# Nine identity products between the first scores and the first weighted sums of a fused attention and long-convolution kernel

## The chip, the cores and the metric

The kernel runs on one core of a Trainium2 chip. Such a core has TensorE (matrix products, which land in PSUM), VectorE and ScalarE (elementwise work; both read PSUM), GpSimd, and SyncE, which here only issues transfers. The traces call these engines PE (PEld for its weight loads), DVE, ACT, POOL and SP. The metric is the device time of the program in microseconds; a profiled execution also gives a span, from the first to the last instruction.

## What is computed

```python
B, S, D = 8, 3136, 256           # z has 64 columns
scores = (1 / S) * (z @ z.T)     # per batch, symmetric
attn = np.maximum(scores, 0) ** 2
x = u * (attn @ v)
proj = x @ w_proj
x1, x2, x3 = proj[..., :D], proj[..., D:2*D], proj[..., 2*D:]
x2_conv = irfft(rfft(x2, axis=1) * rfft(filter_fft, axis=0), n=S, axis=1)
y = x1 * x2_conv * x3
out = y @ w_out
```

## The kernel before

Each batch's 3136 rows are cut into seven chunks of 256 to 512 columns, and into 25 row tiles of up to 128 rows. For each chunk TensorE makes the scores of a few tiles at a time (`score_mm`, a unit), VectorE or ScalarE takes their positive part out of PSUM into R_t (`relu`, lines 1956 and 1958) and squares it into A_t in bf16 (`sq`, lines 1965 and 1967; a few units of the first batch land in buffers named conv_in_t and spec_in_t instead), and TensorE adds the unit's weighted sum of v's rows to the chunk's sum (`weigh`). Since the scores are symmetric, some units are sent through a transposing transfer into M_t and reused for another chunk. When a chunk's sum is whole, VectorE multiplies it by u (line 2012), TensorE projects it, and the convolution runs as two stages of small Fourier products through DRAM. All this is interleaved over the batches.

PSUM is held as four pairs of banks, `ps_t[0]` to `ps_t[3]`; in the order of instructions they are `ps_s_139` to `ps_s_142`. A chunk's running sum keeps a pair until it is whole; scores take one for each unit.

The order is written out by hand. `ORDER` is a string of two-character codes; `Plan.go` takes them one by one and emits the task of that number on its engine. `ENGINES` says which engine takes an elementwise task, `BANKS` which pair a task takes. A code past the last task is no task but a fill, into the pair that the code names:

```python
if k >= len(every):
    self.fill(k - len(every))

def filler():
    p = take_pair()
    for h in range(2):
        i = ident[rows_of(h), :]
        matmul(p[:, h, :], i, i.unsqueeze(1).to_broadcast([N1, 4, P]), start=True, stop=True)
```

A fill thus issues two products of 64 rows of the identity with a repeated copy of the same rows, one in the upper and one in the lower half of the array's rows, each writing one bank of the pair. Nobody reads their result. The kernel before has such fills near its end, and eight identity products over all 128 rows at its start, ahead of everything else on TensorE.

The opening, in which the change lies, makes batch 0's z ready and begins chunk 0. z arrives in pieces of 4, 8 and 13 tiles. Each piece is cast to bf16 twice side by side (`cast`, into xT_t, lines 619 on ScalarE and 623 on VectorE), transposed on TensorE against the identity (`turn`, line 558, into PSUM), and copied out into zT_t (`back`, line 623). After the first piece come the first two score units, each of two tiles with one product for a tile; after the second come the first weighted sums into pair 0, the next scores, and so on. Pair 0 holds the first piece's transposes until VectorE has copied them out, and from the first weighted sum on the running sum of chunk 0. GpSimd meanwhile starts the transfers of v and u, and VectorE also builds the tables of the Fourier stages (percol, gs_t).

Of the kernel before, what the change touches and what calls it, by code (L numbers as in the profile page):

```python
# [11 lines left out]
P = 128  # L12
# [43 lines left out]
    "r}r~2e3Y2f363ks03i3Z3l2g2u372h2w3as13r3B3ss23vs33w2p3b2i2q3c3m2js42k3t3d3n3e3x3f3C2l0c2v0es50d3Q3y3R"
    "s60f3$0g3D3%3)s73j3*s83&3q3Ss93+3;3p3u3<3#3o3(3z3:3=3!3E3,sA3F494G4AsB3>4H3/0lsCsD4B4I0msE0nsF4N4J4C"
    "4K4OsG0o4R4D3-4S3?4E3G4TsH4P444X4UsI4Y3H3T4F3I4b3U454L4csJ4M4Z4i4W4d4msK4n4j0p4e4V3.0q4Q0r4o4a4f4vsL"
    "4k0s4h4p3J4wsM4l4g4x3K3@3L3V4q4?sN464ssO4@3[sP3]50sQ4t514u4[4y520t57473^4]584^sR0usS0v533_4z4_4{594|"
    "0w4}5D4r3{5M4:5EsT4;4~5NsUsV5FsW565O5h555A5l5i5s5B5C5msX5G545JsY5t5wsZ5j5L5#3M5n5P5x5K3N5usa5o5$sb5y"  # L60
    "5H3O5k5)5q5*sc5Q5-3P5%5r5.3|4<5e5&5v5f4=5+3}5(5z3~5<sd485=4!5Ise5/5!5>4#sf4$5?5^0x5p0y5,5_0z5}sg5@5:"
    "5;5{5~5]0!7n7r607osh7vsi7ssjsk7w4%7psl5[5|7t4&7x7z61404(7!sm41sn427%627q7&7u7#437k7)7lso7*7.7(4)7y7/"
    "7$7?7+4*7@sp4>4+7_7,7-7{7:5R7~5Ssq5T7[0#7;sr7<807>7|7]84ss85815U0$5V7^5W0%88827}86st898D8a0&su8E8b83"
    "7=8f8Asv8F878c8m8Bsw8n8C8g8Gsx8o0(8q8h8d0)sy0*8e8r8i0+sz8j8xs!8H8ys#0,8#8k8s8$8V8l8W4,638z0;s$4-644."
    "8t8p8%8u8+s%654/8:8w8,8&8;8v8(5Xs&5Y8-665Z5g8[s(8)8<8]8!8|s)8}8^8=9K8*9L8>8/8~9S8.679T8@0-689Ms*0.0/"
    "8_0<s+0=s,0:5a8{5b8I8X5c0>909U0?5d690@8J9V9Y8K6A9Zs-7m9Ws.9N6B9a0{9O9b91s/9c9P8Y9i9Q9j9F9d9n9Gs:9t8?"
    "9o9R9u9y9k9e9X9f8L9ps;9z6C8M9v9h9q8N9r6D0[6Es<9w9m9!0]9)A1s=6F9*A29s9#0^9$s>9+0_0|9xs?9g0}0~8O109(A3"
    "9l8P928Q8ZAB9Hs@A4A56G9,ACAF93AGs[ADAM6Ts]94s^AH8RANs_9I8SA69-8TAIAQs{9%A7AR9{959|98AOAS96A8AX97A9AJ"
    "AY998UATAUs|9&9AAb9J6HAcAA6I9.AZs}AjAE6JAk6M9/6K6jAL6N6LA)AP9:A*s~6RAd6Ot09BAl6SA:AKAe9CAWAft1A;6P6U"
    "AVt26Q6VAa9Dt3A+6ZAhA[t46W6at59}9;6XA]Ai6b6c6Y9<6dAm9=6ht6A<t76eA,6iA=A{An6zA>A-A|A.A^6k6fB2A#A/9EA$"  # L70
    "6gB66l9~t8B7t9B36pA?Ag6m6qA@A}tAB4BD6nA~9>B06otBBE6r9?B8tCA09@BHA_BFB9BIBQBAB5tDBRB1BJBCBlBvBGA%BmBw"
    "BKBB6sBLBP6t6x9[6yA&tEBS9]tF6u9^B!AoBNB#tGBntHBT6v9_BxB)ApBo6wBOtIB*BqAqB$tJB<tKBMBrB=BUBsB%BtB&C8tL"
    "C9tM6!B>BiB+BuBj6#BzB,B(CACCB-tNCJCD6$6(BytO6)CKB;Ar6%tPCEB/6+As6&6,tQCFBpAtAuCLB:CNtRAvCO6-6:AwB?6*"
    "6.CBtS6;6/CSCHtTB@CT6<CPCICUC5A(B.Ax6=CVCXCWAyCYCMAztUC6CbCQCZCgCR6>ChCnCctVCoCaBVCiCdCrtWCpA!EECsCj"
    "BWCkCeEFBXtXCGBYCfCtEIEGBZEJtYEMCmBaENCqCuBbEKtZ6?EOtaBc6}EQBkB[BdtbERtcClB]tdB^teESEUEXEVEHELCvEPEY"
    "EcEWEBBetfECEdEjBfETEkEZtgthBgEeEaEotiEpB}ElEsEfEbBhEgEtB~EiEmEnC0EuExEq6@E#6[tjEy6]76ErEvtkE$E)B_E*"
    "tlEzB{F1EhC7EwB|E%6^tmE+F2F66_tnF76{E&C1E!C2E(F8F3Cw6|6~toC370F9CxFA71E,7ECyFDtpC4FEFHF4tqFICzE-F5FF"
    "C!trFOC#E{C$E|tsFPFBFSFCFTFJFGC%72C&EDFQFKFZ73FLFaFN74FettFftuFUC(75FRC)E.C*FbFVFlFMFWE/FmtvE:FY77Fn"
    "twC+FgFq78FrFd79E>FXFhFiFkFsE?E}7A7ME@F:Fp7BF;E~txF]7CtyF^tzF<F~t!FcG0t#G2FtG3F_7FE;7GG1t$Fo7HF{E<F|"
    "G4F=F0F>Fu7DG9G5t%GAF?E=F+GE7UF,F@GFGKFjGLE[t&GB7IG6F[GGGME]7Jt(E^7KGHGNt)GIt*GPGXGQF}FvE_G8GYGRG7Fw"  # L80
    "Gut+Fx7NGSt,GTGDGv7OG&GCGJG(GO7PFyGwt-GZG+7cFzG)GxG<C,GyGWF!t.G=Gat/G,G>C^7QG@7RF-G[t:7SGzGVG-t;F#Gb"
    "G]G}G.F.G!G/F$G~G^G#GpF/G_G$F%GqGcH0H2GdH3GUt<GeC-G%C.7LH4t=HAC<HBG*C/H57Tt>H6t?C=C:HXC;t@HYC_C>G;C{"
    "G?DAC?HeC[C@HCt[C]G|HfD0t]H8C|H1D1D3Grt^D4C}G:HlF&C~t_Hm7VF(D57WH9G{F)7XGfHDD6HZ7YD7HpD2GgHgHnt{7Zt|"
    "HqHht}GhHi7aHaHrDQHvt~HEHwHsHzHbHcH!F*HxHSGiHTGsHFH#H)GjHdH*H7GtH$HGH%u0GkHHH-Htu1H.D8H+7bHjD9H@HkH["
    "DBHuH/Hou2DCICH]DGH:u3H=H;u4DHIDu5DJH&HyDKDD7dH(HUDEIE7eDIH,7fGlIMu6IFINDFGmIRH?GnDLHVu7ISH^IOu8IXGo"
# [2021 lines left out]
```

## Time and profile before

| | |
|---|---|
| median of 3 runs | 942.79 us (938.34, 942.79, 945.0) |
| the profiled execution | 942.77 us, its span 940.9 us |
| mean granted clock of TensorE | 0.997 |
| TensorE, VectorE, ScalarE, GpSimd busy | 914.0, 838.7, 819.6, 247.6 us |
| moved by the DMA engines | 170.70 MB, mean 181 GB/s |

Products on TensorE are pipelined and their ends are modelled, so two products that overlap in the two row halves show as two durations of the same time. Idle time of an engine is put down to what ended it. A line such as L553 is that of a helper through which every product goes, so the tile names tell products apart: `ps_s<-zT_t` are scores, `ps_s<-A_t,v_t` weighted sums, `ps_s<-ident,xT_t` transposes of z, and `ps_s<-ident` the eight products at the start or a fill.

### The profile page before, as it was taken

To read this page: it belongs to the slowest core of one execution; us is meant where nothing else is said; L and a number is where in the kernel's file an instruction comes from. 1 tells how busy PE (TensorE), PEld (TensorE's weight loads), DVE (VectorE), ACT (ScalarE), POOL (GpSimd) and SP (SyncE) were. 2 spreads that over 40 slices of the span, in tenths; PEclk is the share of its full clock that TensorE was granted. 3 is DMA by queue.
4 is the path that set the end of the run, shared out by engine and by line. 5 is a ranking of instruction groups with operands and counts; after the bars stand their busy time and mean duration, and the time that the engine had idled before them with its cause. 6 is when DMAs were issued, how large, how long until landed. Compare 5 with 4: busy or idle time off the path is not lost.

```text
span 940.9 us, 30306 instructions
## 1 busy us (share of the span) xinstructions
PE 914.0 (97%) x12425; PEld 555.4 (59%) x12425; DVE 838.7 (89%) x1117; ACT 819.6 (87%) x952; POOL 247.6 (26%) x585
## 2 busy tenths in 40 slices
...
DMA  9899899989999789998999989998999979898867
GB/s 158 155 176 163 141 156 197 185 144 173 169 218 201 151 190 168 206 200 146 192 173 212 177 160 189 178 223 149 200 167 208 224 128 202 202 205 140 207 193 232
DMA packets 331644, 170.70 MB, mean 181 GB/s; under 512 B 242887, under 2 KB 307143, under 8 KB 331505
## 3 DMA queue, kind: packets, MB, share of 16 engines
...
q10 hardware_dynamic: 712, 1.66, 0.6%
q14 instruction: 43, 0.34, 0.2%
...
## 4 chain that ended last, share of the span: by engine, by line
PE 83%; ACT 5%; DMA 5%; DVE 5%; issue 2%; SPq 0%; POOL 0%; DVEq 0%; ACTq 0%; POOLq 0%
PE ps_s L553 82%; DMA M_t<-A_t 3%; ACT R_t L1956 2%; DVE xh L1394 1%; DVE A_t L1967 1%; DMA zn_t<-in_z_dram 1%; ACT A_t L1965 1%; DVE xT_t L2012 1%; DMA A_t<-spec 0%; ACT xh L619 0%; DMA spec<-uT_t 0%; ACT ost_t L619 0%; ACT s_t L619 0%; DVE gs_t L623 0%; ACT R_t L619 0%
## 5 line engine op out<-in xcount | busy, mean ns | idle before, releaser
L553 PE MATMUL ps_s<-A_t,v_t 64*128 64x512 bf16 (+5 forms) x4766 | 515.7, 352 | 1.1 <-DVE A_t L1967 1.0
L553 PEld LDWEIGHTS <-v_t 64*128 64x128 bf16 (+1 forms) x6528 | 305.8, 98 | 185.9 <-PE ps_s L553 19.2
L1956 ACT ACTIVATE R_t<-ps_s 128x1024 f32<-128x1024 f32 (+3 forms) x359 | 336.8, 961 | 50.4 <-PE ps_s L553 47.2
L1965 ACT ACTIVATE A_t<-R_t 128x1024 bf16<-128x1024 f32 (+2 forms) x281 | 271.8, 992 | 12.0 <-DVE R_t L1958 4.9
L1967 DVE SCALAR_TENSOR_TENSOR A_t<-R_t 128x1024 bf16<-128x1024 f32 (+3 forms) x211 | 233.6, 1123 | 17.6 <-ACT R_t L1956 10.3
L553 PE MATMUL ps_s<-zT_t 64*128 64x512 bf16 (+5 forms) x1186 | 191.4, 352 | 4.4 <-DVE gate_t L1293 1.7
L1958 DVE TENSOR_SCALAR R_t<-ps_s 128x1024 f32<-128x1024 f32 (+4 forms) x153 | 170.3, 1124 | 23.7 <-PE ps_s L553 13.3
L676 POOL COPY tick<-A_t 1x1 bf16<-1x1 bf16 x159 | 54.3, 341 | 426.0 <-ACT A_t L1965 262.0
L553 PE MATMUL ps_s<-xT_t,wp 64*128 64x512 bf16 (+3 forms) x976 | 124.3, 352 | 0.5 <-DVE R_t L1958 0.4
L553 PEld LDWEIGHTS <-zT_t 64*128 64x128 bf16 (+1 forms) x1219 | 68.9, 97 | 52.8 <-issue 9.8
L553 PE MATMUL ps_s<-M_t,v_t 64*128 64x512 bf16 (+4 forms) x860 | 96.6, 353 | 1.8 <-DMA M_t<-A_t 1.7
L619 ACT ACTIVATE x_t<-ps_s 128x1024 bf16<-128x1024 f32 (+3 forms) x75 | 69.4, 927 | 20.9 <-PE ps_s L553 18.1
L1394 DVE TENSOR_TENSOR xh<-xh,H 128x1024 bf16<-128x1024 bf16 x120 | 81.8, 685 | 2.9 <-ACT xh L619 2.0
L1293 DVE TENSOR_TENSOR gate_t<-ps_s,x_t 128x512 bf16<-128x512 f32 (+2 forms) x112 | 64.5, 617 | 12.4 <-PE ps_s L553 10.3
L2012 DVE TENSOR_TENSOR xT_t<-ps_s,uT_t 128x512 bf16<-128x512 f32 (+2 forms) x112 | 64.0, 614 | 6.5 <-PE ps_s L553 6.1
L1499 DVE TENSOR_TENSOR yT_t<-ps_s,gate_t 128x1024 bf16<-128x1024 f32 (+2 forms) x53 | 56.9, 1078 | 12.9 <-PE ps_s L553 11.7
L553 PEld LDWEIGHTS <-wp 64*128 64x128 bf16 (+1 forms) x976 | 47.8, 96 | 30.0 <-PE ps_s L553 2.0
L553 PE MATMUL ps_s<-wp,xT_t 64*128 64x256 bf16 (+2 forms) x944 | 64.0, 266 | 0.1
L553 PE MATMUL ps_s<-wo,yT_t 64*128 64x256 bf16 (+2 forms) x904 | 62.3, 266 | 1.0 <-DVE yT_t L1499 0.5
L662 POOL DMA_DIRECT2D un_t<-in_u_dram x112 | 58.1, 519 | 18.5 <-issue 16.0
L688 POOL DMA_DIRECT2D v_t<-in_v_dram x112 | 58.4, 525 | 13.6 <-issue 10.3
L553 PEld LDWEIGHTS <-xT_t 64*128 64x128 bf16 (+1 forms) x944 | 43.5, 97 | 19.1 <-issue 0.6
...
## 6 DMA issues: line engine op xcount, KB each, us to landing
...
```

The costliest lines, as they stand in the source:

```text
L553: got = nc.tensor.matmul(o, *args, **kw)
L619: got = nc.scalar.activation(out_, in_, AF.Copy)
L662: nc.gpsimd.dma_start(out=t[ds(j * N1, N1), lo - t0 : hi - t0, :], in_=x[:, n2 : n2 + hi - lo, :])
L688: nc.gpsimd.dma_start(out=t[ds(j * N1, N1), ds(v_at(a), (b - a) * D)], in_=r[:, n2 + a - lo : n2 + b - lo, :].rearrange("p t d -> p (t d)"),)
L1293: has_read(nc.vector.tensor_tensor(o[:, :, ::-1] if h == 0 else o, p, x, ALU.mult), p)
L1394: nc.vector.tensor_tensor(x[:, 1 - i], x[:, 0], h, ALU.mult)
L1499: has_read(nc.vector.tensor_tensor(yb["y"][:, :, 0:w], p, gates[b, c][:, :, 0:w], ALU.mult), p)
L1956: has_read(nc.scalar.activation(r, p, AF.Relu), p)
L1958: has_read(nc.vector.tensor_single_scalar(r, p, 0.0, ALU.max), p)
L1965: nc.scalar.activation(a, r, AF.Square, scale=1.0 / float(S))
L1967: nc.vector.scalar_tensor_tensor(a, r, inv_s2, r, ALU.mult, ALU.mult)
L2012: has_read(nc.vector.tensor_tensor(x[:, :, ::-1] if h == 0 else x, f, ut, ALU.mult), f)
```

## The change

The only edit is in `ORDER`: the code of a fill into pair 0 (`y<`) is put in six times behind the code `17`, the first scores' second unit, and three times behind `06`, the transposes of the second piece of z. The rest of the string is the same, broken into lines at other places:

```diff
-    "0G0H00010203130I170J1404050K1806150L190716080C1B091G0D1Crx1H0A1A0B1D1L1I1Q0E1M0O1F0F1K1R1N1V1Zry1Wrz"
+    "0G0H00010203130I17y<y<y<y<y<y<0J1404050K1806y<y<y<150L190716080C1B091G0D1Crx1H0A1A0B1D1L1I1Q0E1M0O1F"
...
```

On TensorE, at the first place, before: the second unit of scores (into pair 2, `ps_s_141`), then the eight transposes of z's second piece (into pair 3), of which the first is shown.

```order
L553 MATMUL ps_s_140<-zT_t 128x512
...
L553 LDWEIGHTS zT_t
L553 MATMUL ps_s_141<-zT_t 128x512
L558 LDWEIGHTS xT_t [waits DVE_49]
L558 MATMUL ps_s_142<-ident,xT_t 128x128
```

The same place after it: six fills stand between, each of two loads and two products into pair 0 (`ps_s_139`); the first load and product are shown.

```order
L553 MATMUL ps_s_141<-zT_t 128x512
L553 LDWEIGHTS ident
L553 MATMUL ps_s_139<-ident 128x512
...
L558 LDWEIGHTS xT_t [waits DVE_49]
L558 MATMUL ps_s_142<-ident,xT_t 128x128
```

Twelve products now stand in TensorE's queue ahead of the transposes, none with a wait; the wait for VectorE's cast stays on the first transpose. At the second place, before: the last transpose of that piece, then the first weighted sums into pair 0, which wait for v's transfers and for A_t.

```order
L558 MATMUL ps_s_142<-ident,xT_t 128x128
L553 LDWEIGHTS v_t [waits DMASW0_49]
L553 MATMUL ps_s_139<-A_t,v_t 128x512 [waits DVE_49]
L553 LDWEIGHTS v_t [waits DMASW2_49]
L553 MATMUL ps_s_139<-A_t,v_t 128x512
```

And after it, with three fills ahead of the weighted sums, the first load and product shown:

```order
L558 MATMUL ps_s_142<-ident,xT_t 128x128
L553 LDWEIGHTS ident
L553 MATMUL ps_s_139<-ident 128x512
...
L553 LDWEIGHTS v_t [waits DMASW0_49]
L553 MATMUL ps_s_139<-A_t,v_t 128x512 [waits DVE_49]
```

Six products were put ahead of the weighted sums, into the pair that these overwrite. VectorE's, ScalarE's, GpSimd's and SP's instructions and their order are the same in both.

More of the change, by code (lines that the diff above doesn't have):

```diff
@@ L56 @@
[L56 to L85, printed above, removed]
@@ new lines @@
+    "0F1K1R1N1V1Zry1Wrz1S1P1a1c110M1Xr!1d1U1g0N1b1Er#1h1k1Y1er$1l1o1J1ir%1f1p1m1s1j1=1tr&1qr(1>1]1n1u1}1^"
+    "22r)231r1?1v271_r*1~r+1@241w2B282C2G1-1O1.202L291x2D1T1/r,1y2H0P1[121:1z2M1{1|2Ir-2N2126r.2Pr/2Q2U25"
+    "1!2Vr:0Qr;2R2W2E2A2F2x2K2y2O2(r<2J2)0Rr=r>0S2,1#2S0T2-0h2T1$r?2.0i2X0j2!2z2/r@0U2*r[0k1%1;2Y2#2:1&r]"
+    "0V1<2m2;2>2n1(2^2$2?2%2_r^2o0W2}2@332&2~1)2rr_2{r{342t1*30382+0X2=352s1+312Zr|390Y2a0Z2c1,2b0a2]2<3W"
+    "2|3X3A323g2d2[3h0br}r~2e3Y2f363ks03i3Z3l2g2u372h2w3as13r3B3ss23vs33w2p3b2i2q3c3m2js42k3t3d3n3e3x3f3C"
@@ new lines @@
+    "2l0c2v0es50d3Q3y3Rs60f3$0g3D3%3)s73j3*s83&3q3Ss93+3;3p3u3<3#3o3(3z3:3=3!3E3,sA3F494G4AsB3>4H3/0lsCsD"
+    "4B4I0msE0nsF4N4J4C4K4OsG0o4R4D3-4S3?4E3G4TsH4P444X4UsI4Y3H3T4F3I4b3U454L4csJ4M4Z4i4W4d4msK4n4j0p4e4V"
+    "3.0q4Q0r4o4a4f4vsL4k0s4h4p3J4wsM4l4g4x3K3@3L3V4q4?sN464ssO4@3[sP3]50sQ4t514u4[4y520t57473^4]584^sR0u"
+    "sS0v533_4z4_4{594|0w4}5D4r3{5M4:5EsT4;4~5NsUsV5FsW565O5h555A5l5i5s5B5C5msX5G545JsY5t5wsZ5j5L5#3M5n5P"
+    "5x5K3N5usa5o5$sb5y5H3O5k5)5q5*sc5Q5-3P5%5r5.3|4<5e5&5v5f4=5+3}5(5z3~5<sd485=4!5Ise5/5!5>4#sf4$5?5^0x"
@@ new lines @@
+    "5p0y5,5_0z5}sg5@5:5;5{5~5]0!7n7r607osh7vsi7ssjsk7w4%7psl5[5|7t4&7x7z61404(7!sm41sn427%627q7&7u7#437k"
+    "7)7lso7*7.7(4)7y7/7$7?7+4*7@sp4>4+7_7,7-7{7:5R7~5Ssq5T7[0#7;sr7<807>7|7]84ss85815U0$5V7^5W0%88827}86"
+    "st898D8a0&su8E8b837=8f8Asv8F878c8m8Bsw8n8C8g8Gsx8o0(8q8h8d0)sy0*8e8r8i0+sz8j8xs!8H8ys#0,8#8k8s8$8V8l"
+    "8W4,638z0;s$4-644.8t8p8%8u8+s%654/8:8w8,8&8;8v8(5Xs&5Y8-665Z5g8[s(8)8<8]8!8|s)8}8^8=9K8*9L8>8/8~9S8."
+    "679T8@0-689Ms*0.0/8_0<s+0=s,0:5a8{5b8I8X5c0>909U0?5d690@8J9V9Y8K6A9Zs-7m9Ws.9N6B9a0{9O9b91s/9c9P8Y9i"
@@ new lines @@
+    "9Q9j9F9d9n9Gs:9t8?9o9R9u9y9k9e9X9f8L9ps;9z6C8M9v9h9q8N9r6D0[6Es<9w9m9!0]9)A1s=6F9*A29s9#0^9$s>9+0_0|"
+    "9xs?9g0}0~8O109(A39l8P928Q8ZAB9Hs@A4A56G9,ACAF93AGs[ADAM6Ts]94s^AH8RANs_9I8SA69-8TAIAQs{9%A7AR9{959|"
+    "98AOAS96A8AX97A9AJAY998UATAUs|9&9AAb9J6HAcAA6I9.AZs}AjAE6JAk6M9/6K6jAL6N6LA)AP9:A*s~6RAd6Ot09BAl6SA:"
+    "AKAe9CAWAft1A;6P6UAVt26Q6VAa9Dt3A+6ZAhA[t46W6at59}9;6XA]Ai6b6c6Y9<6dAm9=6ht6A<t76eA,6iA=A{An6zA>A-A|"
+    "A.A^6k6fB2A#A/9EA$6gB66l9~t8B7t9B36pA?Ag6m6qA@A}tAB4BD6nA~9>B06otBBE6r9?B8tCA09@BHA_BFB9BIBQBAB5tDBR"
@@ new lines @@
+    "B1BJBCBlBvBGA%BmBwBKBB6sBLBP6t6x9[6yA&tEBS9]tF6u9^B!AoBNB#tGBntHBT6v9_BxB)ApBo6wBOtIB*BqAqB$tJB<tKBM"
+    "BrB=BUBsB%BtB&C8tLC9tM6!B>BiB+BuBj6#BzB,B(CACCB-tNCJCD6$6(BytO6)CKB;Ar6%tPCEB/6+As6&6,tQCFBpAtAuCLB:"
+    "CNtRAvCO6-6:AwB?6*6.CBtS6;6/CSCHtTB@CT6<CPCICUC5A(B.Ax6=CVCXCWAyCYCMAztUC6CbCQCZCgCR6>ChCnCctVCoCaBV"
+    "CiCdCrtWCpA!EECsCjBWCkCeEFBXtXCGBYCfCtEIEGBZEJtYEMCmBaENCqCuBbEKtZ6?EOtaBc6}EQBkB[BdtbERtcClB]tdB^te"
+    "ESEUEXEVEHELCvEPEYEcEWEBBetfECEdEjBfETEkEZtgthBgEeEaEotiEpB}ElEsEfEbBhEgEtB~EiEmEnC0EuExEq6@E#6[tjEy"
@@ new lines @@
+    "6]76ErEvtkE$E)B_E*tlEzB{F1EhC7EwB|E%6^tmE+F2F66_tnF76{E&C1E!C2E(F8F3Cw6|6~toC370F9CxFA71E,7ECyFDtpC4"
+    "FEFHF4tqFICzE-F5FFC!trFOC#E{C$E|tsFPFBFSFCFTFJFGC%72C&EDFQFKFZ73FLFaFN74FettFftuFUC(75FRC)E.C*FbFVFl"
+    "FMFWE/FmtvE:FY77FntwC+FgFq78FrFd79E>FXFhFiFkFsE?E}7A7ME@F:Fp7BF;E~txF]7CtyF^tzF<F~t!FcG0t#G2FtG3F_7F"
+    "E;7GG1t$Fo7HF{E<F|G4F=F0F>Fu7DG9G5t%GAF?E=F+GE7UF,F@GFGKFjGLE[t&GB7IG6F[GGGME]7Jt(E^7KGHGNt)GIt*GPGX"
+    "GQF}FvE_G8GYGRG7FwGut+Fx7NGSt,GTGDGv7OG&GCGJG(GO7PFyGwt-GZG+7cFzG)GxG<C,GyGWF!t.G=Gat/G,G>C^7QG@7RF-"
@@ new lines @@
+    "G[t:7SGzGVG-t;F#GbG]G}G.F.G!G/F$G~G^G#GpF/G_G$F%GqGcH0H2GdH3GUt<GeC-G%C.7LH4t=HAC<HBG*C/H57Tt>H6t?C="
+    "C:HXC;t@HYC_C>G;C{G?DAC?HeC[C@HCt[C]G|HfD0t]H8C|H1D1D3Grt^D4C}G:HlF&C~t_Hm7VF(D57WH9G{F)7XGfHDD6HZ7Y"
+    "D7HpD2GgHgHnt{7Zt|HqHht}GhHi7aHaHrDQHvt~HEHwHsHzHbHcH!F*HxHSGiHTGsHFH#H)GjHdH*H7GtH$HGH%u0GkHHH-Htu1"
+    "H.D8H+7bHjD9H@HkH[DBHuH/Hou2DCICH]DGH:u3H=H;u4DHIDu5DJH&HyDKDD7dH(HUDEIE7eDIH,7fGlIMu6IFINDFGmIRH?Gn"
+    "DLHVu7ISH^IOu8IXGoIHDMIIIYIgu9H<DNITDOIhuADPuBIUH>IJIVIKuCH_IiDRI#ILDSIZIQI97gIAuDI$IWIaDTIbI(uE7hI)"
@@ new lines @@
+    "DUIPI/uFI%7iHII:uGHJIdDVI*I=HLHKI>IfI+IGHMIeI;I]IjHWHNI^uHI?I}J27juII~uJJ3I&I_DWIkI{I-I|DZDXHODaIyIc"
+    "uKIzHPI.J0HQI<uLDbJ7DYH{J8JEJ4uMJFJIH|DcJJI@HRDdH~H}DeJ9I0DfI[JGJAK*JBJ1K+J5I1I,DgJ6DhK.JKuNI2K/DiK<"
+    "I3K=K,uOIBuPJDK@JCK:I4JHuQuRK[uSK>K_K}uTK~JLuUK{K-K]uVDjuWDrJMK;L0L3I5K|K?K&L4K(L1LAK^LBI6LFL5uXLGL2"
+    "I7L6LJuYLCL7LKuZI8IlL9LHLDDkImLLLODlInuaLPLEDmDzLSLILTLMubLQLXLuLYLNDnLvucLUIoDoLZudLVDpIpDsLwueDtIq"
+    "LRD*D!DuLWL8LzD#L!ufD$L)D<LaL*ugDqL-IrL#uhL.LxIsL$LyLbL%ItL&I!L>IuuiL+L?LpL]LqIvL(IwL/ujL^JNIxL,M0L@"
```

148 lines of the change are left out of this document (69 added, 79 removed).

## The prediction

> **What bounds the kernel now.** I read the page first (shares, the slices, the chain that ended last), then the opening by windows of one microsecond, then the timeline of each engine there, and last the chain of waits behind the opening.
>
> ```profile
> span 940.9 us, 30306 instructions
> ...
> PE 914.0 (97%) x12425; PEld 555.4 (59%) x12425; DVE 838.7 (89%) x1117; ACT 819.6 (87%) x952; POOL 247.6 (26%) x585
> ...
> DMA  9899899989999789998999989998999979898867
> ...
> PE 83%; ACT 5%; DMA 5%; DVE 5%; issue 2%; SPq 0%; POOL 0%; DVEq 0%; ACTq 0%; POOLq 0%
> ```
>
> TensorE is busy 97% of the span and carries 83% of the chain, and the DMA engines are near full all the way. The change acts on under 10 of 941 us, so the question is what happens in the opening and how much of it reaches the end. The windows give busy time by engine, then the granted clock (PEclk), the DMA share and GB/s:
>
> ```profile
> 9.00:10.00 1.00, 0.29 (x4) 0.20 (x4) 1.00 (x2) 0.89 (x1) 0.47 (x1) 0.96 1.13 213
> 10.00:11.00 1.00, 1.00 (x8) 0.34 (x6) 1.00 (x3) 0.02 (x1) 0.64 (x2) 0.50 1.13 215
> ...
> 13.00:14.00 1.00, 1.00 (x12) 0.38 (x9) 0.64 (x2) 0.96 (x2) 0.84 (x2) 0.84 1.17 205
> ```
>
> A clock of 0.96 in the first window is 0.08 us at half speed, so the clock fell at 9.92; 0.84 in the last is 0.32 us at half speed, so it came back at 13.32. In these 3.4 us TensorE streams what takes 1.7 us at full clock. That is the most the change can win. The timeline of TensorE (start, us, engine, line, operation, count, and in brackets the idle time before):
>
> ```profile
> 1.72 3.59 PE L553 MATMUL ps_s<-ident 128*128 128x512 bf16 x8 [1.72 <-DVE tick L715]
> ...
> 6.26 0.70 PE L553 MATMUL ps_s<-zT_t 64*128 64x512 bf16 x4 [0.52 <-DVE zT_t L623]
> 8.46 0.62 PE L558 MATMUL ps_s<-ident,xT_t 128*128 128x128 bf16 x8 [1.50 <-DVE xT_t L623]
> 9.79 0.96 PE L553 MATMUL ps_s<-A_t,v_t 64*128 64x512 bf16 x4 [0.71 <-DVE A_t L1967]
> 10.52 1.09 PE L553 MATMUL ps_s<-zT_t 64*128 64x512 bf16 x4
> 11.37 1.09 PE L553 MATMUL ps_s<-A_t,v_t 64*128 64x512 bf16 x4
> 12.40 0.93 PE L558 MATMUL ps_s<-ident,xT_t 128*128 128x128 bf16 x7
> ...
> 13.71 0.59 PE L553 MATMUL ps_s<-zT_t 64*128 64x512 bf16 x4
> ```
>
> Four score products take 0.59 us at 13.71, 1.09 at 10.52 and 0.70 at 6.26. The last is close to the fast one, so the clock was up for most of it: it rose a little after 6.26, near 6.5. The eight warm-up products (3.59 / 8 = 449 ns each, double the fast rate) ran slow, though no window shows a low clock there; for that stretch I go by the durations. The idle times before 8.46 and 9.79 are the two places where the fills go. Between 6.55 and the fall TensorE did little:
>
> ```profile
> 6.55:9.96 3.41, 1.20 (x14) 0.65 (x12) 3.34 (x11) 3.10 (x4) 1.87 (x4) 0.99 1.10 197
> ...
> 3.10:6.50 3.40, 2.88 (x12) 1.08 (x12) 2.55 (x18) 1.64 (x4) 3.40 (x8) 1.00 1.03 207
> ...
> 920.00:923.40 3.40, 2.06 (x50) 1.40 (x52) 1.77 (x2) 0.60 (x1) 1.03 (x2) 1.00 0.81 227
> ```
>
> With 1.20 of 3.41 us busy the clock fell; with 2.88 of 3.40 it had risen; with 2.06 of 3.40 near the end it stayed up. So the line lies, as far as these rows tell, between 1.2 and about 2.1 us in such a stretch.
>
> **The change part by part.** It adds 18 weight loads and 18 products to TensorE, two for each fill, and moves nothing on the other engines or on SP's and POOL's queues. Price of a fill, from the fills near the end (same shape, same line):
>
> ```profile
> 895.79 0.38 PE L553 MATMUL ps_s<-ident 64*128 64x512 bf16 x2
> ...
> 914.63 1.24 PE L553 MATMUL ps_s<-ident 64*128 64x512 bf16 x10
> ```
>
> One fill is two products in the two row halves, which end together after 0.38 us; five take 1.24, so each further one costs (1.24 - 0.38) / 4 = 0.215 us. At half clock two pairs start 11.37 - 10.52 = 0.85 us apart, 0.425 each.
>
> *Six fills behind the scores.* The scores end at 6.96, and their stream 0.38 - 0.215 = 0.16 earlier, at 6.80. Six fills stream to 6.80 + 6 x 0.215 = 8.09 and end at 8.25. The transposes that follow could start at 8.46 and not earlier, because their input is cast on VectorE until then:
>
> ```profile
> 7.65 0.76 DVE L623 CAST xT_t<-ost_t 128x512 bf16<-128x512 f32 x2
> 8.32 0.29 DVE L914 SCALAR_TENSOR_TENSOR gs_t<-gs_t 128x128 f32<-128x128 f32 x1
> 8.52 1.22 DVE L1967 SCALAR_TENSOR_TENSOR A_t<-R_t 128x1024 bf16<-128x1024 f32 x1
> ```
>
> The cast ends at 8.41. Cost of the six: nothing, with 0.2 us to spare; if that cover goes (a slower fill, an earlier cast), each further fill delays the transposes by its full length.
>
> *Three fills behind the transposes.* Eight transposes stream about 8 x 0.055 = 0.45 us (their 0.62 less a tail of 0.16 to 0.2), to 8.91; three fills stream to 9.56 and end at 9.72. The first weighted sum waits for A_t, made by VectorE until 8.52 + 1.22 = 9.74. Cost: nothing, again with under 0.1 to 0.2 us to spare.
>
> *Their waits.* The fills have none of their own: pair 0 was last read by the zT copy for which the scores ahead of them already wait, and the weighted sums that overwrite it follow on the same engine. Nothing new waits for a fill except through TensorE's order.
>
> *The clock.* With the fills the stretch 6.55 to 9.96 has 1.20 + 9 x 0.215 = 3.1 of 3.41 us busy, above both cases in which the clock was or stayed up. I take it that the clock stays up. TensorE then has its first four weighted-sum products done 0.43 us after 9.79; the scores at 10.52 still wait for the zT copy, stream 0.43 instead of 0.85, and the rest follows: 0.43 for the sums at 11.37, then the seven transposes at about 11.4 instead of 12.40, held now by their own cast. TensorE is about 1 us early there. Who can use it?
>
> ```profile
> 10.26 1.14 DVE L623 CAST xT_t<-ost_t 128x448 bf16<-128x448 f32 x2
> 11.31 1.22 DVE L1958 TENSOR_SCALAR R_t<-ps_s 128x1024 f32<-128x1024 f32 x1
> 13.36 0.62 DVE L623 COPY zT_t<-ps_s 128x896 bf16<-128x896 bf16 x1 [0.84 <-PE ps_s L558]
> ...
> 25.64 1.23 DVE L1958 TENSOR_SCALAR R_t<-ps_s 128x1024 f32<-128x1024 f32 x1 [0.56 <-ACT R_t L1956]
> ```
>
> ```profile
> 10.98 1.12 ACT L619 ACTIVATE xT_t<-ost_t 128x320 bf16<-128x320 f32 x4 [1.08 <-DMA ost_t<-in_z_dram]
> 12.01 1.00 ACT L1956 ACTIVATE R_t<-ps_s 128x1024 f32<-128x1024 f32 x1
> 12.91 1.05 ACT L1965 ACTIVATE conv_in_t<-R_t 128x1024 bf16<-128x1024 f32 x1
> 14.19 4.84 ACT L1956 ACTIVATE R_t<-ps_s 128x1024 f32<-128x1024 f32 x5 [0.24 <-PE ps_s L553]
> ```
>
> The same from 14.19 to 30.5 as one window (busy us of TensorE, its weight loads, VectorE, ScalarE, GpSimd):
>
> ```profile
> 14.19:30.50 16.31, 14.74 (x131) 6.51 (x131) 15.71 (x19) 16.20 (x18) 3.91 (x9) 1.00 1.26 156
> ```
>
> VectorE gets its copy at 12.53 instead of 13.36 and wins 0.84. ScalarE waits at 10.98 for a z transfer that the change doesn't move, runs without a break to 13.96, and loses only 0.24 us to TensorE; from 14.19 to 30.5 it is busy 16.20 of 16.31 us. So ScalarE sets the pace there, and VectorE's 0.56 us of waiting for it at 25.64 will merely be longer. The opening wins 0.24 us, between the ends of 0 and 1.7.
>
> *Behind the opening.* TensorE is the bound again, but transfers cut in; a piece of the chain that ended last (start, us), and the window around it:
>
> ```profile
> 69.84 10.03 DMA M_t<-A_t
> ```
>
> ```profile
> 30.00:100.00 70.00, 68.57 (x707) 35.79 (x705) 55.86 (x79) 54.02 (x62) 26.09 (x58) 1.00 1.05 164
> ```
>
> The chain hangs 10 us on a mirror transfer, with the DMA share at 1.05. If that transfer is late because of the queue ahead of it, some of the 0.24 goes there; I keep it whole, since its source is written by an engine that is early too. Sum: 942.77 - 0.24 = 942.5. The profiled execution took 942.77 us (its span of 940.9 and 1.9 around it), which is the median 942.79 of the three runs.
>
> **The rivals.**
> 1. *The fills don't hold the clock.* For it: the two idle times are 1.50 and 0.71 us, and the eight slow warm-up products show that the clock follows work only after some 3 us, so where the stretch begins may differ in another execution. Against: 3.1 of 3.41 us busy. Then nothing moves: 942.8. [...]
> 2. *The fills hold up the transposes* (slower). Place: the six behind the scores. They have 8.46 - 6.80 = 1.66 us, so it decides from 1.66 / 6 = 277 ns a fill. If the clock is still low there, a fill takes 425: the scores stream until 7.11, six fills until 9.66, and the transposes start 1.2 us late; at half clock they and three fills more (8 x 0.107 + 3 x 0.425 = 2.1) bring the first weighted sum to 11.8 instead of 9.79. ScalarE then waits for scores: up to 2.0 us, 944.8. Against it: 0.70 us for the scores at 6.26.
> 3. *More is won than ScalarE lets me see*: VectorE's 0.84 us passes on, or all 1.7: 941.9 to 941.1. Against: ScalarE's 16.20 of 16.31.
>
> **How the numbers follow.** Forecast 0.45, rival 1 0.27, rival 2 0.12, rival 3 0.14, anything else 0.02. All lie between 941.1 and 944.8, less than the three runs differ (938.34 to 945.0). So the range comes from the scatter and the bounds: 938.34 less rival 3's 0.84 gives 937.5, 945.0 and about half of rival 2's 2.0 give 946.0; the prediction is 942.5. One per cent is 9.4 us, about what a measurement of this kernel can tell from no change; no case comes near it. Faster by over 1% 0.02, within 1% 0.96, slower by over 1% 0.02, for what the scatter and the unknown may do.
>
> **What would show it.** Right: in the windows from 10 to 14 a clock of 1.00; in TensorE's timeline the transposes still at about 8.46 and the first weighted sum at 9.79; VectorE's zT copy near 12.5; ScalarE's row of five relus near 13.96 and still unbroken. Rival 1: the clock of 0.50 stays, or falls elsewhere. Rival 2: transposes after 8.7 with TensorE busy ahead of them. Wrong would be a change of 3 us or more in the median, which none of these steps pays for.

## The result and the profile after

| | before | after | ratio, 95% interval |
|---|---|---|---|
| median, 22 runs each | 942.19 us (937.28 to 951.98) | 947.40 us (938.93 to 956.33) | 1.0051 [1.0028, 1.0075] |
| the profiled execution | 942.77 us, span 940.9 | 946.33 us, span 944.5 | |

The change costs about half a per cent in this timing, where 942.5 us, next to no change, was forecast. Ratios here and below leave out runs more than 1.5% above the fastest of their kernel (two of the 22 after, and further down also single runs of 5328, 1185 and 1056 us). The page of the kernel after (the same four lines that the prediction shows of before):

```profile
span 944.5 us, 30342 instructions
...
PE 915.9 (97%) x12443; PEld 557.5 (59%) x12443; DVE 838.3 (89%) x1117; ACT 819.4 (87%) x952; POOL 249.1 (26%) x585
...
DMA  9999889989999699999999989999999979898868
...
PE 82%; DMA 8%; DVE 3%; ACT 3%; issue 2%; POOL 1%; SPq 0%; DVEq 0%; ACTq 0%; POOLq 0%
```

TensorE is busy 1.9 us longer (nine fills of 0.215 us would be as much), VectorE and ScalarE as long as before. The span is 3.6 us longer, and the chain that ended last has gone from 5% to 8% on transfers. The opening, by windows (columns as before: busy time by engine, PEclk, DMA share, GB/s):

```profile
9.00:10.00 1.00, 1.00 (x10) 0.28 (x6) 1.00 (x2) 0.64 (x1) 0.74 (x2) 1.00 1.07 205
10.00:11.00 1.00, 1.00 (x10) 0.31 (x8) 1.00 (x3) 0.21 (x1) 0.27 (x2) 1.00 1.13 214
13.00:14.00 1.00, 0.96 (x10) 0.50 (x10) 1.00 (x2) 1.00 (x2) 0.89 (x2) 1.00 1.16 202
6.55:9.96 3.41, 3.11 (x32) 1.25 (x26) 3.34 (x10) 3.08 (x4) 2.25 (x5) 1.00 1.11 206
14.19:30.50 16.31, 14.31 (x128) 6.25 (x126) 15.46 (x18) 16.23 (x18) 4.49 (x10) 1.00 1.33 125
```

The clock that stood at 0.50 from 10 to 13 us is now 1.00 throughout, and the stretch that had 1.20 of 3.41 us busy has 3.11. TensorE's timeline after:

```profile
1.72 3.30 PE L553 MATMUL ps_s<-ident 128*128 128x512 bf16 x8 [1.72 <-DVE tick L715]
...
6.01 0.61 PE L553 MATMUL ps_s<-zT_t 64*128 64x512 bf16 x4 [0.52 <-DVE zT_t L623]
6.45 1.46 PE L553 MATMUL ps_s<-ident 64*128 64x512 bf16 x12
8.20 0.62 PE L558 MATMUL ps_s<-ident,xT_t 128*128 128x128 bf16 x8 [0.30 <-DVE xT_t L623]
8.76 0.82 PE L553 MATMUL ps_s<-ident 64*128 64x512 bf16 x6
9.54 0.61 PE L553 MATMUL ps_s<-A_t,v_t 64*128 64x512 bf16 x4
...
28.66 0.61 PE L553 MATMUL ps_s<-zT_t 64*128 64x512 bf16 x4 [1.28 <-DVE xT_t L2012]
```

The same products of TensorE before, at the end of the opening:

```profile
29.25 0.76 PE L553 MATMUL ps_s<-zT_t 64*128 64x512 bf16 x4 [1.12 <-DVE xT_t L2012]
```

Both rows of fills fit in this execution: after the six TensorE still waits 0.30 us for the cast, after the three it doesn't wait at all. At 28.66 the kernel is 0.59 us ahead of before. So the opening is no slower here, and the loss comes later. The table compares the start of the same product of TensorE in the two profiles, at some times of before:

| at (us of before) | 30 | 70 | 90 | 150 | 210 | 270 | 330 | 510 | 570 | 870 | 930 |
|---|---|---|---|---|---|---|---|---|---|---|---|
| after minus before, us | -0.58 | -0.58 | +1.14 | +1.14 | +2.65 | +2.64 | +7.00 | +7.09 | +4.37 | +4.95 | +3.66 |

The lead is kept exactly for 40 us and then goes in steps: at 80, at 178, and in several between 270 and 320 us. At the first, TensorE waits for a mirror transfer, before and after:

```profile
79.92 0.60 PE L553 MATMUL ps_s<-M_t,v_t 64*128 64x512 bf16 x4 [0.91 <-DMA M_t<-A_t]
```

```profile
81.06 0.61 PE L553 MATMUL ps_s<-M_t,v_t 64*128 64x512 bf16 x4 [2.63 <-DMA M_t<-A_t]
```

At the second, SP's queue issues the same transposing transfers in another rhythm (start, us of issue), before:

```profile
163.57 2.45 SPq L1657 DMA_TRANSPOSE zT_t<-zd_t  x1
166.14 1.25 SPq L1602 DMA_TRANSPOSE uT_t<-un_t  x1
...
168.07 1.45 SPq L1885 DMA_TRANSPOSE M2e_t<-A_t  x1
```

and after:

```profile
165.16 1.27 SPq L1657 DMA_TRANSPOSE zT_t<-zd_t  x1
166.53 3.60 SPq L1602 DMA_TRANSPOSE uT_t<-un_t  x1
...
170.82 1.31 SPq L1885 DMA_TRANSPOSE M2e_t<-A_t  x1
```

VectorE waits for the last of them to have read A_t, and TensorE then for VectorE (two engines' timelines after; before, neither of these two had a wait there):

```profile
177.79 1.23 DVE L1967 SCALAR_TENSOR_TENSOR A_t<-R_t 128x1024 bf16<-128x1024 f32 x1 [1.65 <-DMA M2e_t<-A_t]
```

```profile
180.47 0.41 PE L553 MATMUL ps_s<-xh,TZ 64*64 64x512 bf16 x4 [1.35 <-DVE xh L1399]
```

In the third stretch the clock falls for one window as well, of which before had none there; 3.41 us at half clock are 1.7 us:

```profile
301.55:304.96 3.41, 3.41 (x28) 2.19 (x26) 1.36 (x2) 2.28 (x3) 2.74 (x6) 0.50 1.17 231
```

In this pair of profiles, all of this is far behind the edit, on instructions that are the same in both kernels.

### The profile page after: what moved, and what is told of

Same layout as the page of the kernel before. It is cut to its first block, busy times and chain, and to the rows that moved or that the text cites. A ratio compares the mean times of both kernels' runs of the same rounds, so it can differ in the third digit from the quotient of the medians.

```text
span 944.5 us, 30342 instructions
## 1 busy us (share of the span) xinstructions
PE 915.9 (97%) x12443; PEld 557.5 (59%) x12443; DVE 838.3 (89%) x1117; ACT 819.4 (87%) x952; POOL 249.1 (26%) x585
## 3 DMA queue, kind: packets, MB, share of 16 engines
q8 instruction: 97, 1.59, 0.7%
## 4 chain that ended last, share of the span: by engine, by line
PE 82%; DMA 8%; DVE 3%; ACT 3%; issue 2%; POOL 1%; SPq 0%; DVEq 0%; ACTq 0%; POOLq 0%
PE ps_s L553 82%; DMA M_t<-A_t 4%; DMA uT_t<-un_t 1%; ACT R_t L1956 1%; ACT A_t L1965 1%; DMA un_t<-in_u_dram 1%; DMA A_t<-spec 1%; DVE R_t L1394 1%; DMA v_t<-in_v_dram 1%; DVE xh L1394 0%; DMA M2e_t<-A_t 0%; DVE xT_t L2012 0%; DMA zn_t<-in_z_dram 0%; ACT ost_t L619 0%; DVE yT_t L1499 0%
```

## The experiments

Every kernel below computes the whole reference: fills, wide or thin, write PSUM that nobody reads. Ratios are to the kernel before, timed in turn with each kernel on the same chip.

**Is it the timing? (two kernels.)** The first theory was that a program that is 0.6 us early meets its transfers at other moments. A clearing of the first chunk's xT_t, in front of the product with u (line 2012), costs VectorE 0.48 us and takes the lead away again. It was put into the change and into the kernel before:

```diff
 xt["t"] = xT_p.tile()
+for _ in range(1 if b == 0 and c == 0 else 0):
+    nc.vector.memset(xt["t"][:], 0.0)
```

> The changed kernel with one more VectorE instruction: the first chunk's xT is cleared (about 0.49 us) ahead of the product with u. From there on everything should run within 0.1 us of the kernel before, instead of 0.58 us ahead of it. Theory of the shift (the loss comes since all later work starts 0.6 us earlier and meets the transfers otherwise): the loss goes, ratio to before 0.998 to 1.002. Theory of the instructions (18 more weight loads and products in TensorE's stream move its instruction fetches): the loss stays, 1.003 to 1.007. Theory of chance (the later loss hangs on nothing that the change fixes): anywhere, with a spread of runs like that of both kernels.

> The kernel before with the same clearing of the first chunk's xT: no fill, the clock dip of the opening stays, all later work starts 0.5 us later. Theory of the shift: if any shift against the order for which the numbers were set costs, 1.003 or more; if only an earlier start costs, 1.0005 (0.5 us). Theory of the instructions: 1.0005, TensorE's stream is that of before.

Measured: the change with the clearing 1.0038 [1.0004, 1.0071], the kernel before with it 0.9998 [0.9967, 1.0029]. In the first the opening ran as in the change, with the fills in place, and at 30 us the kernel was 0.90 us behind the one before, not ahead (0.1 us at most was expected; the scores that wait for ScalarE's relu were late as well, at 13.83 us where the change has them at 12.87):

```profile
7.01 1.46 PE L553 MATMUL ps_s<-ident 64*128 64x512 bf16 x12
8.46 0.62 PE L558 MATMUL ps_s<-ident,xT_t 128*128 128x128 bf16 x8
9.01 0.82 PE L553 MATMUL ps_s<-ident 64*128 64x512 bf16 x6
```

So the loss doesn't need the lead, and in the kernel before a delay (0.57 us at 30 us) makes no loss. The timing theory has lost its ground, though the two delays are not the same.

**Is it the fills' work? (two kernels.)** One kernel has only the six fills behind the scores, 24 instructions instead of 36 (this diff and the next are against the change):

```diff
-    "0G0H00010203130I17y<y<y<y<y<y<0J1404050K1806y<y<y<150L..."
+    "0G0H00010203130I17y<y<y<y<y<y<0J1404050K1806150L..."
```

The other has all nine, but each product 32 columns wide in place of 512, so that the same 36 instructions do hardly any work (0.30 and 0.26 us in their profile, against 1.46 and 0.82 of the full ones):

```diff
+plan.fills += 1
 for h in range(2):
     i = ident[rows_of(h), :]
-    matmul(p[:, h, :], i, i.unsqueeze(1).to_broadcast([N1, 4, P]), start=True, stop=True)
+    if plan.fills <= 9:
+        matmul(p[:, h, 0:32], i, i[:, 0:32], start=True, stop=True)
+    else:
+        matmul(p[:, h, :], i, i.unsqueeze(1).to_broadcast([N1, 4, P]), start=True, stop=True)
```

> Only the six fills behind the first scores, none behind the transposes. The stretch in question has about 1.2 + 1.3 = 2.5 us of work in 3.4, so the clock should stay up, and the later work should start about 0.6 us early as with all nine. Theory of the shift: 1.003 to 1.007 as with nine. Theory of the instructions: another amount, since the stream is moved by 24 instructions instead of 36.

> All nine fills, but each product 32 columns wide instead of 512: the same number of instructions at the same places, with next to no work in them. The clock should dip in the opening as before where the stretch begins likewise, so that later work starts as before (within 0.1 us). Theory of the shift: no loss, 0.998 to 1.002. Theory of the instructions: the loss stays, 1.003 to 1.007.

Measured: six fills 1.0037 [1.0011, 1.0063]; nine thin ones 1.0012 [0.998, 1.0044]. The thin fills did not hold the clock; the same windows in their profile:

```profile
9.00:10.00 1.00, 0.85 (x10) 0.29 (x12) 1.00 (x3) 0.43 (x1) 0.20 (x1) 0.50 1.09 204
10.00:11.00 1.00, 1.00 (x7) 0.39 (x7) 1.00 (x3) 0.00 (x0) 0.70 (x2) 0.50 1.17 223
```

The thin one's 1.0012 lies where the timing theory had it (0.998 to 1.002), below the 1.003 or more of a loss through the instructions, and its interval leaves both open. But its profile shows the same wait at 178 us as the change, without the fills' work and without the clock that they hold:

```profile
178.19 0.41 PE L554 MATMUL ps_s<-xh,TZ 64*64 64x512 bf16 x4 [1.69 <-DVE xh L1404]
```

**Is it the place in the instruction stream? (eight kernels.)** What the kernels with this wait share is 24 to 36 more instructions ahead of all others on TensorE. The page lists what carries those instructions, a queue of its own, whose packets it counts in the time of the same 16 DMA engines as all transfers (packets, MB, share); the line is the same before and after:

```profile
q8 instruction: 97, 1.59, 0.7%
```

1.59 MB in 97 packets are 16.4 KB each, and 1.59 MB over TensorE's 24,850 weight loads and products (12,425 of each) are 64 bytes for one: a packet would be 256 instructions. The trace of before agrees: between the first packet, at 23.4 us, and the last, at 932.7, TensorE began 24,538 loads and products, 255.6 for each of the 96 steps. So I take a packet for a block of TensorE's list, and its start for the time at which the block is read. Then 36 more instructions ahead put every later read 36 instructions earlier in the program, and the two traces have it so: from the third on, the 95 reads stand at the same count of loads and products before and after, the 36 added ones counted (2 fewer after in the mean, singly between 82 fewer and 66 more). Around the wait at 178 us, on the time scale of before, the trace has blocks read at 164.2, 173.4, 180.0, 188.7 and 199.3 us before, and at 161.0, 174.3, 178.9, 187.2 and 197.0 after. At the first of these five TensorE had begun 3,283 loads and products before, and 3,260 after with the 36 added ones among them: about the same place in the list, and so an earlier one in the program. The theory: the schedule was settled with the reads at one set of places, and at another set they cut into the transposing transfers on which the chain hangs. It says that the same thin fills cost nothing near the end, as much at 139 or 187 us as in the opening, and nothing if there are 256 instructions of them. The four edits stand in this order: nine thin fills at 884 us, at 139 us (into pair 1), at 187 us, and 64 in the opening.

```diff
-    "...y,lyl+y-q8y...."
+    "...y,lyl+y<y<y<y<y<y<y<y<y<y-q8y...."
```

```diff
-    "...8>8/8~9S8.67..."
+    "...8>8/8~y=y=y=y=y=y=y=y=y=9S8.67..."
```

```diff
-    "...A@A}tAB4BD6nA~..."
+    "...A@A}tAB4y<y<y<y<y<y<y<y<y<BD6nA~..."
```

```diff
-    "0G0H00010203130I170J1404050K1806150L..."
+    "0G0H00010203130I17y<y<y<y<y<y<y<y<y<y<y<y<y<y<y<y<y<y<y<y<y<y<y<y<y<y<y<y<y<y<y<y<y<y<y<y<y<y<y<y<0J1404050K1806y<y<y<y<y<y<y<y<y<y<y<y<y<y<y<y<y<y<y<y<y<y<y<y<150L..."
```

> The kernel before with nine thin fills (18 loads and 18 products 32 columns wide, about 0.6 us) near its end, at about 884 us; nothing is added ahead of that. Theory of the stream's position (36 instructions more shift all later blocks of 256 instructions, and so the places in the program at which TensorE's 16 KB instruction fetches fall among the transfers): ahead of 884 us all fetches fall where they did, no TensorE wait on xh at about 178 us, and the ratio is 0.999 to 1.002. Rival, the mere number of instructions or the size of the program: 1.003 to 1.005 as with the thin fills in the opening.

> The same nine thin fills at about 139.5 us, into pair 1. The opening is that of before with its clock dip. Theory of the stream's position: the fetch that fell at about 164 us falls at about 161, the xh wait at 178 is there (1.3 to 1.7 us), the ratio is 1.002 to 1.006. Rival, something in the opening (the fills between the scores and the sums, or the pair that they write): no wait at 178, ratio 0.999 to 1.002.

> The same nine thin fills at about 187 us, behind the place of that wait. Theory of the stream's position: no xh wait at 178; the later fetches are moved, so the part of the loss that falls behind 187 us may stay: ratio 1.000 to 1.004, below that of the thin fills at 139 us. Rival of chance: the wait at 178 comes and goes without regard to where the fills stand.

> 64 thin fills at the two places of the change (40 and 24): 256 instructions, one whole block of the stream. They should delay the opening by some 2 to 3 us, since they take about 0.07 us each and the gaps are 1.5 and 0.7. Theory of the stream's position: behind the opening the fetches fall where they did in the kernel before (one fetch more in the opening), no xh wait at 178, and the ratio is the delay alone, 1.002 to 1.004, with the span from 50 us on as in before. Theory of the number of instructions: loss on top of the delay, 1.006 or more, and the wait at 178 is there.

Measured: at the end 0.9994 [0.9965, 1.0022]; at 139 us 1.0037 [0.9999, 1.0074]; at 187 us 1.0040 [1.0006, 1.0074]; 256 instructions 1.0006 [0.9978, 1.0034]. A whole block costs nothing that can be measured, and the fewer ones at 139 or 187 us came out 0.4% slower (the first interval just holds 1). Three things came out otherwise than the theory had them: with the nine at 139 us the blocks were displaced at 178 us too, and its profile has no wait there; the nine at 187 us did not lose less than those at 139; and the 256 instructions, expected to delay the opening by 2 to 3 us, delayed it by 0.10 us at 30 us.

**The change's own fills with a whole block, a displacement for a part of the program, and other displacements.** In the first kernel the nine full fills stand at their places and 55 thin ones beside them, where TensorE is idle, 256 instructions in all. In the second the nine thin fills of the opening are followed by 55 at 139 us (at the place shown above), so that only the first 139 us are displaced. The third and fourth have 32 (20 and 12) and 16 (10 and 6) thin fills at the change's two places. The four edits in this order, against the kernel before:

```diff
-    "0G0H00010203130I170J1404050K1806150L..."
+    "0G0H00010203y?y?y?y?y?y?y?y?y?y?y?y?y?y?y?y?y?y?130I17y<y<y<y<y<y<0J1404050K1806y<y<y<150L..."
...
-    "...~1+@241w2B282C..."
+    "...~1+@241wy?y?y?y?y?y?y?y?y?y?y?y?y?y?y?y?y?y?y?y?y?y?y?y?y?y?y?y?y?y?y?y?y?y?y?y?y?2B282C..."
```

```diff
-    "0G0H00010203130I170J1404050K1806150L..."
+    "0G0H00010203130I17y<y<y<y<y<y<0J1404050K1806y<y<y<150L..."
...
-    "...8>8/8~9S8.67..."
+    "...8>8/8~y=y=y=y=y=y=y=y=y=y=y=y=y=y=y=y=y=y=y=y=y=y=y=y=y=y=y=y=y=y=y=y=y=y=y=y=y=y=y=y=y=y=y=y=y=y=y=y=y=y=y=y=y=y=y=9S8.67..."
```

```diff
-    "0G0H00010203130I170J1404050K1806150L..."
+    "0G0H00010203130I17y<y<y<y<y<y<y<y<y<y<y<y<y<y<y<y<y<y<y<y<0J1404050K1806y<y<y<y<y<y<y<y<y<y<y<y<150L..."
```

```diff
-    "0G0H00010203130I170J1404050K1806150L..."
+    "0G0H00010203130I17y<y<y<y<y<y<y<y<y<y<0J1404050K1806y<y<y<y<y<y<150L..."
```

> The change's nine full fills at their places, and 55 thin ones (32 columns wide) beside them, 18 ahead of the first scores and 37 in TensorE's idle 1.3 us at 27.4, so that 256 instructions are added in all, as many as one fetch of TensorE's instructions holds. Theory (where the fetches fall decides): behind 30 us the fetches stand as in the kernel before, the loss of 4 us is gone, and the opening's 0.6 us may be kept: ratio 0.997 to 1.001. Rival (the fills' work, the clock held up by them, or an earlier rest of the program is what costs): ratio 1.003 or more, as in the change.

> The nine thin fills of the opening (36 instructions), and 55 more at 139 us (220), so that the fetches are displaced up to 139 us only and stand as before behind it. Theory: the loss of the change arises where the fetches are displaced, and most of the program is not: ratio 0.999 to 1.002, of which up to 1.5 us (0.0016) are the 110 thin products themselves. Rival (something that the opening sets off costs the time, wherever the fetches stand later): 1.003 or more.

> 32 thin fills in the opening, 128 instructions, half of what one fetch holds. Theory in its wide form (the kernel's order was settled with the fetches where they stood, and any other place costs): ratio 1.003 to 1.005. In its narrow form (a displacement by 24 to 36 happens to hit a bad place): 0.998 to 1.002. Rival (more instructions cost more): 1.005 or more.

> 16 thin fills in the opening, 64 instructions, a quarter of what one fetch holds. Theory in its wide form: ratio 1.003 to 1.005; in its narrow form 0.998 to 1.002, and this one and the one with 128 may then differ.

Measured: full fills with 256 instructions 0.9975 [0.9946, 1.0004], as the theory expects and outside what the rival expects; 128 instructions 1.0022 [0.9991, 1.0054] and 64 instructions 1.0013 [0.9979, 1.0048], between the two forms of the theory. With the full block the opening was as in the change, at full clock:

```profile
9.00:10.00 1.00, 1.00 (x10) 0.20 (x4) 1.00 (x3) 0.52 (x1) 0.68 (x2) 1.00 1.03 198
10.00:11.00 1.00, 1.00 (x10) 0.31 (x8) 1.00 (x3) 0.00 (x0) 0.59 (x2) 1.00 1.11 213
```

and its page counts one block more:

```profile
q8 instruction: 98, 1.61, 0.7%
```

The kernel displaced up to 139 us came out at 1.0030 [0.9996, 1.0064], which is what the rival expected and not what the theory did (0.999 to 1.002). Its TensorE timeline has a reason why the number need not speak for the rival:

```profile
139.36 1.54 PE L556 MATMUL ps_s<-ident 64*128 64x32 bf16 x110 [0.33 <-ACT R_t L1963]
...
145.26 0.63 PE L556 MATMUL ps_s<-A_t,v_t 64*64 64x512 bf16 x8 [1.04 <-issue]
```

The 110 thin products take 1.54 us as expected, but they come with a wait of 0.33, and 1.04 us later on in which TensorE waited for nothing that the profile shows: 2.9 us, or 0.0031 of the time, as much as all of its loss. This is a reading after the result and from one profile; no run has the 55 thin fills at 139 us alone. Its stretch from 172 to 320 us lost nothing against before.

**Beside the change itself (three kernels on one chip).** The change once more; the change with seven thin fills at 27.4 us (64 instructions in all), whose edit follows; the kernel with full fills and 256 instructions once more.

```diff
-    "0G0H00010203130I170J1404050K1806150L..."
+    "0G0H00010203130I17y<y<y<y<y<y<0J1404050K1806y<y<y<150L..."
...
-    "...~1+@241w2B282C..."
+    "...~1+@241wy?y?y?y?y?y?y?2B282C..."
```

> The change itself once more, as the yardstick on this chip: 1.003 to 1.007 of the kernel before, as when it was first timed.

> The change's nine full fills at their places and seven thin ones in TensorE's idle time at 27.4 us: 64 instructions are added instead of 36. Theory (the place in the stream decides, and with 64 added instructions the thin fills cost nothing): 0.998 to 1.002. Rival (the fills' work or what the opening sets off costs): the same as the change beside it, 1.003 to 1.007.

> The kernel with nine full fills and 256 added instructions once more. Theory: 0.997 to 1.001 again, about 4 us under the change beside it; if its first result was luck, 1.003 or more. Whether it also beats the kernel before is open; together the two results would show a gain of 0.2%.

Measured: the change 1.0021 [0.9989, 1.0053], less than the first time and not clear of no loss; with 64 instructions 1.0029 [1.0001, 1.0057], where the theory expected no loss and its rival 1.003 or more; with 256 instructions 1.0001 [0.9971, 1.0031]. So 64 instructions cannot be called free: thin ones came out at 1.0013, full ones at 1.0029, and the two intervals overlap.

**All together.** The last column is what TensorE's products lose against before in the profile between 172 and 210 us, where the wait at 178 us lies:

| kernel | instructions added | stands in the blocks behind 30 us | ratio | lost from 172 to 210, us |
|---|---|---|---|---|
| the change, twice | 36 | displaced | 1.0051, 1.0021 | 1.51, 0.93 |
| change and clearing | 36 | displaced | 1.0038 | 1.78 |
| six fills | 24 | displaced | 1.0037 | 1.74 |
| nine thin | 36 | displaced | 1.0012 | 1.88 |
| thin at 139 us | 36 | displaced from 139 us on | 1.0037 | -0.01 |
| thin at 187 us | 36 | displaced from 187 us on | 1.0040 | 0.22 |
| thin, 128 | 128 | displaced | 1.0022 | 1.43 |
| thin, 64 | 64 | displaced | 1.0013 | 1.20 |
| full fills, 64 | 64 | displaced | 1.0029 | 0.86 |
| before and clearing | 0 | as before | 0.9998 | -0.01 |
| thin at 884 us | 36 | as before up to 884 us | 0.9994 | -0.02 |
| thin, 256 | 256 | as before | 1.0006 | 0.00 |
| full fills, 256, twice | 256 | as before | 0.9975, 1.0001 | -0.01, 0.00 |
| 36, then 220 at 139 us | 256 | as before from 139 us on | 1.0030, 0.9999 without its 2.9 us | -0.01 |

The ten displaced results lie between 1.0012 and 1.0051, their mean is 1.0030; the five that stand as before, the last row left out, lie between 0.9975 and 1.0006, mean 0.9995. The gap between 1.0006 and 1.0012 is small beside the intervals, half of the ten have intervals that hold 1, and the last row's 1.0030 as it was measured falls among the displaced. The fills' work and the clock that they hold divide the kernels differently and don't sort the ratios: full fills stand on both sides, thin ones too.

One rival is left in these ratios: the clock. Runs of the same kernel are slower where their mean granted clock is lower (of the 128 runs of the kernel before in the ratios of the experiments, the 43 with 0.996 or more took 941.0 us in the mean, the 42 with 0.993 or less 946.2), and the kernels did not all get the same one. Over the runs in the ratios it was 0.9942 to 0.9945 for the kernel before, 0.9919 and 0.9925 for the thin fills at 139 and 187 us, and 0.9972 for the thin ones with 256 instructions. As an estimate, take from each run the time that its clock cost (its span, times one less the clock). Then the nine timings of displaced kernels in these batches are 0.7 to 5.5 us slower than the kernel before on the same chip, 3.0 in the mean. Four of the five that stand as before are 0.3 to 0.7 us slower, but the thin ones with 256 instructions 3.0, and the last row 3.3. So the two groups stay apart in the mean and not in every kernel; whether a displaced stream also lowers the clock, these runs don't tell. The change's own loss isn't the clock: its second timing had 0.9959 beside 0.9945 for the kernel before, and by the same estimate it was 3.0 us slower.

## Why the prediction was wrong

- *The price of a fill* (0.215 us each behind the first) was right: six took 1.46 us, and 0.38 + 5 x 0.215 is 1.455.
- *Six fills behind the scores* and *three behind the transposes*, at no cost: right in the first profile of the change. The forecast spare time of 0.2 us behind the six was 0.30, and the weighted sums followed the three without a pause. In the second profile of the change rival 2 came true in a small way. The four scores took 1.03 us, close to the 1.09 of the slow clock, the six fills 1.72, and the transposes began 0.28 us later than before, the weighted sums 0.16:

```profile
6.26 1.03 PE L553 MATMUL ps_s<-zT_t 64*128 64x512 bf16 x4 [0.52 <-DVE zT_t L623]
7.09 1.72 PE L553 MATMUL ps_s<-ident 64*128 64x512 bf16 x12
8.74 0.62 PE L558 MATMUL ps_s<-ident,xT_t 128*128 128x128 bf16 x8
9.29 0.82 PE L553 MATMUL ps_s<-ident 64*128 64x512 bf16 x6
9.95 0.59 PE L553 MATMUL ps_s<-A_t,v_t 64*128 64x512 bf16 x4
```

ScalarE did not feel it: its row of five relus began at 13.98, unbroken, where the prediction had 13.96.

- *The clock* stays up with 3.1 of 3.41 us busy: right (3.11 measured, at 1.00 from 9 to 14 us). Rival 1 did not come true in the change, and did in the kernel with thin fills, whose clock was 0.50 there. But the line "between 1.2 and about 2.1 us" is none that busy time alone draws. In the kernel with thin fills at 187 us the clock fell behind a stretch with 2.42 of 3.40 us busy, and in the kernel before with the clearing it stayed up behind one with 1.56 (the first two lines are the stretch and what follows it in the one, the last two in the other):

```profile
906.20:909.60 3.40, 2.42 (x42) 1.07 (x39) 3.40 (x7) 3.38 (x7) 1.79 (x4) 1.00 0.28 59
909.66:913.07 3.41, 3.34 (x58) 2.69 (x61) 3.41 (x6) 3.34 (x7) 0.84 (x2) 0.50 0.93 227
...
26.50:29.90 3.40, 1.56 (x16) 0.74 (x14) 3.25 (x6) 3.37 (x4) 0.30 (x2) 1.00 1.14 202
29.90:33.30 3.40, 2.88 (x26) 1.34 (x27) 3.40 (x5) 2.82 (x4) 2.16 (x4) 1.00 1.00 130
```

- *The opening wins 0.24 us*: the mechanism was right in this pair of profiles. ScalarE stayed the bound, busy 16.23 of 16.31 us, and its row of five relus begins at 13.67 in place of 14.19, without the wait of 0.24 for TensorE:

```profile
11.81 1.00 ACT L1956 ACTIVATE R_t<-ps_s 128x1024 f32<-128x1024 f32 x1
...
13.67 4.64 ACT L1956 ACTIVATE R_t<-ps_s 128x1024 f32<-128x1024 f32 x5
```

Of these 0.52 us, 0.20 lie ahead: the relu in front of the row, which follows the cast of a z piece that ScalarE waits for (1.08 us for its transfer, until 10.98, before; 1.15 us, until 10.79, in the change, with no releaser in the profile), is at 11.81 in place of 12.01. The other 0.32 are between the two. That the change wins this in other executions isn't shown. In all sixteen other profiles of this case the row begins 1.84 to 1.94 us behind that relu, whether the clock fell in the opening or not; only that of before has 2.18. So the row's start goes with that cast, and by my reading with the z transfer: it lies at 13.67 to 14.78 us in the nine profiles whose clock stayed up there, at 14.02 to 14.41 in the eight whose clock fell.

The scores began 0.25 us earlier in the change (6.01 in place of 6.26) for a reason that isn't the change: the eight warm-up products ahead of the fills took 3.30 us and not 3.59. In four profiles these eight took 3.30, 3.42, 3.59 and 3.60 us (the change, full fills with 256 instructions, before, the change with the clearing); what sets it isn't shown.

- *Behind the opening* the 0.24 was kept whole "since its source is written by an engine that is early too". The transfer named there did arrive late, and TensorE waited 2.63 us in place of 0.91. But that place varies without the change: in the second profile of the change it lost 0.25 us in place of 1.72, and in ten of the other fourteen profiles, displaced or not, 1.08 us were won there. It is no cost of the change that I can show.
- *The step that failed* is the first sentence of the part on the change: 18 loads and 18 products, which move "nothing on the other engines or on SP's and POOL's queues". That holds for the order of instructions. What 36 more instructions move is the place in the program at which each later block of TensorE's list is read (at 164.2 us with 3,283 loads and products begun before, at 162.1 with 3,260 after), over DMA engines that were near full all the way (80% or more in 36 of the 40 slices before). This term was put at nothing and stood in no rival. It measured +0.30%, about 2.8 us, as the mean of the ten displaced results, and 1.0051 and 1.0021 in the two timings of the change. In the traces 0.9 to 1.9 us of it are the wait at 178 us; where the rest arises stays open. "Wrong would be a change of 3 us or more in the median, which none of these steps pays for" was the right alarm.
- *The range* took its scatter from three runs, 938.34 to 945.0. In 22 runs the kernel before went from 937.28 to 951.98.

What is shown, and what is not. Ten timings with a displaced stream lose 0.30% in the mean, and five in which it stands as before lose nothing in the mean (0.9995). One place where displacement costs is found in the traces: the wait at 178 us, in eight of the nine profiles with displaced blocks there and in none of the eight without, worth 0.9 to 1.9 us. The grouping was formed on the first eight kernels. Of the seven timed after it (the last two batches) six fall on its two sides; the seventh, displaced up to 139 us only, fits only if its 2.9 us are taken off.

How a read that comes elsewhere holds up the transposing transfers at 178 us is inferred from the changed lengths of their issues. These lengths alone don't settle it, since uT_t's issue was long also in a kernel without the wait (2.85 us, thin fills at 884 us). The rest of the loss stays open. It lies in stretches that differ from profile to profile, 262 to 320 us above all, where the change lost 4.36 and 2.78 us in its two profiles and the other displaced ones between -0.15 and 4.85, but four of the six profiles that stand as before there lost 1.7 to 2.5 as well. One profile for each kernel doesn't divide it. No kernel was tried in which a single read is moved and all others stay, and none with a whole block and 36 more.
